# p's loads on a second queue, idle turns and an early table in the prologue; the last unit by hand in two halves and stored in eight pieces

## The chip, the core and the metric

The kernel runs on one core of one Trainium2 chip. The core has five engines that work side by side, each through its own instructions in order: TensorE (PE; its weight loads are shown as PEld), VectorE (DVE), ScalarE (ACT), GpSimd (POOL) and SyncE (SP), which here only issues DMAs. An engine that issues a DMA spends time of its own queue on that, and the 16 DMA engines of the core move the data afterwards. The metric is the time of one execution on the device in microseconds (us); lower is better. TensorE's clock has two levels, 1.2 and 2.4 GHz; the profile shows the granted one as 0.5 or 1.0.

## What is computed

Attention through a packed set of 32 queries, and two feed-forward layers behind it, all in float32:

```python
def sm_attn(qq, kk, vv):
    s = scale * np.matmul(qq, kk.transpose(0, 1, 3, 2))
    s = s - np.max(s, axis=-1, keepdims=True)
    a = np.exp(s)
    a = a / (np.sum(a, axis=-1, keepdims=True) + 1e-09)
    return np.matmul(a, vv)
p_packed = sm_attn(p, k, v)
x = sm_attn(q, p_packed, p_packed)
...
h = x @ w_in;  x = (h * np.cos(h)) @ w_out
...
h = x @ w_in2
P = a[0] + a[1]*h + a[2]*h**2 + a[3]*h**3
Q = 1 + abs(b[0])*abs(h) + abs(b[1])*h**2
out = (P / (Q + 1e-6)) @ w_out2
```

q, k and v are 8 batches x 8 heads x 576 x 64, p is 8 x 8 x 32 x 64; 4608 tokens of 512 features then pass through the two layers with 2048 hidden features.

## The kernel before

The program has three stages.

**The prologue** (up to about 100 us) makes the packed attention. For each batch b, k comes in as one block of 1152 KB (`load_k`, two buffers), v as two pairs of loads (`load_v`, three buffers `vx_p`), and p once: eight loads of 64 KB, one for each head, into `px`, which lies in the third v buffer (line 157). VectorE turns k (`prep`, `prep_ext`, lines 192 to 206) and p (`turn_p`, line 177) so that TensorE can multiply them: `s1` (line 232) makes the scores of a batch in 80 small matmuls, `top` the row maxima on VectorE, `expo` the exponential on ScalarE, `et` turns the result with TensorE by means of `ident` (line 289), `pv` multiplies it by v, and `ppt` and `packed` put it where it is needed. The loop over c (line 566) interleaves these for successive batches, together with the conversion of the first weights (`load_conv`, `conv_in`). The order is written out by hand: `tc.manual_schedule` for ScalarE, VectorE and TensorE (line 153) and for SP (line 156) makes each of these engines keep the order of the program. On SP that is: k's block 0, the eight loads of p, k's block 1, the first block of w_in, the two loads of v's block 0, then k's block 2, which waits until `prep_ext(0)` has freed its buffer, and so on. POOL keeps the scheduler's order; it clears the padding of the v buffers, that of the third one when p has been turned (line 574).

**The first layer** (to 808 us) is ordered by hand too (`slot`, line 912): TensorE makes h (line 726) and y (line 788) in turn, while weights are converted and packed beside it.

**The second layer** works through 144 units (t, f): 9 blocks t of 512 tokens, and 16 groups f of 128 hidden features; they are counted 0 to 143 here. A unit is `mm_h2` (12 matmuls of 512 columns into one PSUM bank, line 1051), `chain2` (line 1078: six passes of ScalarE and six of VectorE over 128 x 512, which form P, and 1/Q by a reciprocal square root, its square and one correction), `finish_g2` (line 1063: the product g is split into a high part on ScalarE, line 1069, and a low part on VectorE, line 1075), and `mm_o` (line 1128: for each of four groups s of 128 tokens three matmuls, high x high, high x low, low x high, into one of four PSUM banks). `mm_o` of a unit comes two units after its h. Here the order is a scheduler's, which works from a simulated timeline. In the last block the outputs of the last two units are added pair by pair (`mm_o(142, 143)`), and `store_last` copies each group of 128 x 512 out of PSUM, one half by ScalarE (line 1119) and one by VectorE (line 1120), and writes two groups in eight DMAs of 64 KB, issued by SP and ScalarE in turn (line 1123): sixteen in all.

Of the kernel before, what the change touches and what calls it, by code (L numbers as in the profile page):

```python
# [9 lines left out]
F32 = mybir.dt.float32  # L10
F32R = mybir.dt.float32r
U32 = mybir.dt.uint32
AF = mybir.ActivationFunctionType
ALU = mybir.AluOpType
# [6 lines left out]
def pack_attention_moe_moe_kernel(  # L21
# [14 lines left out]
    nc = tc.nc  # L36
    B, H, S, D = q.shape
    M = p.shape[2]
    NT, DM = out.shape
# [4 lines left out]
    CB = S // 16  # L44
# [4 lines left out]
    NFC = DFF // 128  # L49
    NKD = DM // 128  # L50
    NDB = D // 32
    scale = 1.0 / math.sqrt(D)
    RND = 1.5 * 2.0 ** 23
    INV2PI = 1.0 / (2.0 * math.pi)
    PASSES = ((0, 0), (0, 1), (1, 0))
# [56 lines left out]
    ident = const.tile([128, 128], F32, name="ident")  # L112
    pick = const.tile([128, 2, 2, M], F32, name="pick")
    par = const.tile([128, 8], F32, name="par")
    coef = const.tile([128, 8], F32, name="coef")
    one = const.tile([128, 1], F32, name="one")
# [3 lines left out]
    QC = 1.0 + 1e-6  # L120

    if True:

        a_p = [ctx.enter_context(tc.tile_pool(name=f"a{i}", bufs=1)) for i in range(2)]
# [3 lines left out]
        wb_p = ctx.enter_context(tc.tile_pool(name="wb", bufs=1, side="right"))  # L128
        cv_p = ctx.enter_context(tc.tile_pool(name="cv", bufs=1, side="right"))
# [4 lines left out]
        ps0 = e0p.enter_context(tc.tile_pool(name="ps0", bufs=1, space=PSUM))  # L134
# [3 lines left out]
        def load_k(b):  # L138
            kx_t[b] = wk.tile([128, CB, D], F32, tag="kx", bufs=2, name="kx")
            nc.sync.dma_start(out=kx_t[b], in_=k[b].rearrange("h (j c) d -> (h j) c d", c=CB))  # L140
# [16 lines left out]
        px = vx_p[2].rearrange("p h c -> p (h c)")[:, 0:B * 2 * D].rearrange("p (b u d) -> p b u d", b=B, u=2)  # L157
# [5 lines left out]
        load_k(0)  # L163
        for h in range(H):
            rg, u = divmod(h, 2)
            nc.sync.dma_start(out=px[32 * rg:32 * rg + 32, :, u], in_=p[:, h].rearrange("b m d -> m b d"))
        load_k(1)
        nc.vector.memset(coef[:, 6:7], RND)
        nc.vector.memset(coef[:, 7:8], math.pi / 2.0)
        nc.vector.memset(par[:, 6:7], QC)  # L170
        qb = par[:, 6:7]
        make_identity(nc, ident)
        nc.vector.tensor_copy(out=pick, in_=ident.rearrange("p (a u m) -> p u a m", a=2, u=2))
        wl = wi_p.tile([128, B * H * 32 + 128], F32, name="wl")
        nc.gpsimd.memset(wl, 0.0)
# [342 lines left out]
        for fq in (0, 2, 1, 3):  # L518
            pool, tag, bufs = (wi_p, "w1i", 2) if fq % 2 else (wb_p, "wb", 8)
# [151 lines left out]
        NB = NT // 512  # L671
        w2_s, x_t, pools = {}, {}, {}
# [8 lines left out]
        def load_x(t):  # L681
            for x in range(2):
                for k2 in range(2):
                    if x and k2:
                        pool, tag, bufs = (const, "pp", 1) if t % 2 else (pools["a"], "x", 1)
                    else:
                        pool, tag, bufs = (pools["b"], f"x{x}{k2}", 1) if t % 2 else (cv_p, "st64", 3)
                    s = pool.tile([128, 2, 512], F32R, tag=tag, bufs=bufs, name=f"x{x}{k2}")
                    nc.sync.dma_start(
                        out=s.bitcast(F32),  # L690
                        in_=yd[x][2 * k2:2 * k2 + 2, :, 512 * t:512 * t + 512].rearrange("k p s -> p k s"),
                    )
                    for i in range(2):
                        x_t[t, x, 2 * k2 + i] = s[:, i]
# [132 lines left out]
        ps1 = ctx.enter_context(tc.tile_pool(name="ps1", bufs=1, space=PSUM, **RW))  # L827
# [207 lines left out]
        psh2 = ctx.enter_context(tc.tile_pool(name="psh2", bufs=1, space=PSUM, **RW))  # L1035
# [6 lines left out]
        slots2 = [(t, f) for t in range(NB) for f in range(NFC)]  # L1042
        h2_t, g2_t, o_t = {}, {}, {}

        def mm_h2(n):
            t, f = slots2[n]
            ps = psh2.tile([128, 512], F32, tag="h2", bufs=4, name="h2")
            i = 0
            for kk in range(NKD):
                for a, c in PASSES:  # L1050
                    nc.tensor.matmul(  # L1051
                        out=ps,
                        lhsT=w2_s[f][:, 0, a, 128 * kk:128 * kk + 128],
                        rhs=x_t[t, c, kk],
                        start=(i == 0),
                        stop=(i == 3 * NKD - 1),
                    )
                    i += 1
            h2_t[n] = ps
# [3 lines left out]
        def finish_g2(n, part):  # L1063
            if n not in gf and n not in g2_t:
                return
            if part == 0:
                gt = gf[n]
                gh = pools["a"].tile([128, 512], F32R, tag="g2h", bufs=3, name="g2h")
                nc.scalar.activation(out=gh, in_=gt, func=AF.Copy)  # L1069
                g2_t[n] = [gh, None]  # L1070
            else:
                gt = gf.pop(n)
                gh = g2_t[n][0]
                gl = pools["a"].tile([128, 512], F32R, tag="g2l", bufs=3, name="g2l")
                nc.vector.tensor_tensor(out=gl, in0=gt, in1=gh.bitcast(F32), op=ALU.subtract)  # L1075
                g2_t[n][1] = gl
# [25 lines left out]
        def store(t, s):  # L1102
            ot = a_p[0].tile([128, DM], F32, tag=("ah", "al")[s % 2], bufs=2, name="ot")
            nc.scalar.activation(out=ot, in_=o_t[s], func=AF.Copy)
            w = 0
            while w < 4:
                b, cc = divmod((512 * t + 128 * s) // 32 + w, C)
                m = min(4 - w, C - cc)
                nc.sync.dma_start(
                    out=out[b * S:b * S + S, :].rearrange("(j c) e -> c j e", c=CB)[2 * cc:2 * (cc + m)],  # L1110
                    in_=ot[32 * w:32 * (w + m), :],
                )
                w += m

        def store_last(t, ss):
            ot = pools["b"].tile([128, 2, DM], F32, tag=f"x0{ss[0] // 2}", bufs=1, name="ol")
            hd = DM // 2
            for i, s in enumerate(ss):
                nc.scalar.activation(out=ot[:, i, 0:hd], in_=o_t[s][:, 0:hd], func=AF.Copy)
                nc.vector.tensor_copy(out=ot[:, i, hd:DM], in_=o_t[s][:, hd:DM])  # L1120
            for w in range(8):
                b, c = divmod((512 * t + 128 * ss[0]) // 16 + w, CB)
                (nc.sync, nc.scalar)[w % 2].dma_start(
                    out=out[b * S:b * S + S, :].rearrange("(j c) e -> j c e", c=CB)[:, c:c + 9:8],
                    in_=ot[16 * w:16 * w + 16],
                )

        def mm_o(*ns):
            for n in ns:
                if slots2[n][1] == 0:  # L1130
                    for s in range(4):
                        o_t[s] = ps1.tile([128, DM], F32, tag=f"y{s}", name=f"o{s}")
            t, f = slots2[ns[-1]]
            ends = t == NB - 1 and f == NFC - 1
            for ss in ((0, 1), (2, 3)) if ends else ((0,), (1,), (2,), (3,)):
                for n in ns:
                    t, f = slots2[n]
                    for s in ss:
                        for i, (a, c) in enumerate(PASSES):
                            nc.tensor.matmul(  # L1140
                                out=o_t[s],
                                lhsT=g2_t[n][a][:, 128 * s:128 * s + 128],
                                rhs=w2_s[f][:, 1, c],
                                start=(f == 0 and i == 0),
                                stop=(f == NFC - 1 and i == 2),
                            )
                if ends:
                    store_last(t, ss)
                elif f == NFC - 1:
                    store(t, ss[0])  # L1150
            for n in ns:
                del g2_t[n]

        for n, (t, f) in enumerate(slots2):
            mm_h2(n)
            chain2(n)
            if f == 2 and 0 < t < NB - 1:
                load_x(t + 1)
            if n >= 2:
                mm_o(n - 2)  # L1160
        finish_g2(len(slots2) - 1, 0)
        finish_g2(len(slots2) - 1, 1)
        mm_o(len(slots2) - 2, len(slots2) - 1)


# [28 lines left out]
```

## Time and profile before

| what | value |
|---|---|
| median of 3 runs (lowest to highest) | 1599.57 us (1599.39 to 1599.61) |
| the profiled execution: its own time | 1599.44 us |
| the profiled execution: span from first to last instruction | 1597.6 us |
| TensorE busy | 1541.5 us, 96% of the span |
| VectorE busy | 1252.9 us, 78% |
| ScalarE busy | 1173.3 us, 73% |
| GpSimd busy | 164.6 us, 10% |
| mean granted clock of TensorE | 0.988 |
| DMA: moved, mean rate | 175.40 MB, 110 GB/s |

All times in what follows are microseconds from the span's start. "Idle before" is the time that an engine stood before a group of instructions, and the arrow names what ended it. In the chain of waits each piece is the work that the next one waited for; "issue" is time in which the engine waited for nothing that the profile shows. A DMA share is the mean busy share of the 16 DMA engines; where packets overlap it can exceed 1.

### The profile page before, as it was taken

What the parts mean: (1) busy time and instruction counts of PE and PEld (TensorE: products, weight loads), DVE (VectorE), ACT (ScalarE), POOL (GpSimd) and SP (SyncE); (2) the same over time, 40 slices, a digit from 0 to 9 for tenths busy, and PEclk for the clock granted to TensorE, in tenths of its full rate; (3) what the DMA queues carried; (4) which work ended last, traced back from release to release, by engine and by line L of the source; (5) the groups of instructions that cost most, each with busy time, mean ns of one, the idle gap of its engine ahead of it and who ended that gap; (6) DMA issues with size and microseconds to landing.
All of it is one profiled execution on the core that took longest, in us unless ns stands there. A gap on an engine that the chain in (4) does not pass through costs nothing.

```text
span 1597.6 us, 26583 instructions
## 1 busy us (share of the span) xinstructions
PE 1541.5 (96%) x10096; PEld 1328.5 (83%) x10096; DVE 1252.9 (78%) x1897; ACT 1173.3 (73%) x1979; POOL 164.6 (10%) x126
## 2 busy tenths in 40 slices
PE   5789999999999999999999999999999999999997
PEld 3455679999999999999988888888888888888886
DVE  6768787777878787779668888888888888889886
ACT  3566776777777777777677778777787778788875
POOL 1124331020202020203100000000000000000000
PEclk8889999999999999999999999999999999999999
DMA  9747773434434443345970102010111010020000
GB/s 353 242 172 255 231 241 124 125 124 125 128 121 132 120 137 120 126 146 177 312 263 31 49 1 74 7 54 26 54 27 53 27 53 27 5 75 1 27 1 26
DMA packets 98863, 175.40 MB, mean 110 GB/s; under 512 B 11568, under 2 KB 44848, under 8 KB 97712
## 3 DMA queue, kind: packets, MB, share of 16 engines
q1 hardware_dynamic: 98352, 173.19, 32.9%
q8 instruction: 79, 1.29, 0.3%
q10 hardware_dynamic: 384, 0.52, 0.1%
q14 instruction: 48, 0.39, 0.1%
HBM read 113.31 MB, written 60.36 MB: 109 GB/s over the span
## 4 chain that ended last, share of the span: by engine, by line
PE 87%; DVE 5%; ACT 3%; DMA 2%; issue 2%; SPq 0%; POOL 0%; DVEq 0%; POOLq 0%; ACTq 0%
PE h L1051 25%; PE o L1140 24%; PE y L788 22%; PE h L726 11%; PE s L221 2%; PE w L383 1%; DMA vx<-in_v_dram 1%; DVE cvf L86 1%; PE w L357 1%; DVE cvf L91 1%; ACT r L757 1%; ACT r L756 0%; PE pv L302 0%; DVE kT L197 0%; DMA st<-in_moe_w_out_dram 0%
## 5 line engine op out<-in xcount | busy, mean ns | idle before, releaser
L788 PE MATMUL y<-gh,w1o 128*128 128x288 f32 x2048 | 433.9, 297 | 0.9 <-DVE yl L71 0.9
L1051 PE MATMUL h<-x,w 128*128 128x512 f32 x1728 | 406.0, 389 | 0.0
L1051 PEld LDWEIGHTS h<-x,w 128*128 128x128 f32 x1728 | 324.2, 188 | 67.2
L788 PEld LDWEIGHTS y<-gh,w1o 128*128 128x128 f32 x2048 | 334.6, 188 | 6.9 <-issue 5.2
L788 PE MATMUL y<-gl,w1o 128*128 128x288 f32 x1024 | 302.3, 295 | 2.8 <-DVE gl L71 2.5
L1140 PE MATMUL o<-w,g2h 128*128 128x512 f32 x1152 | 292.9, 389 | 1.4 <-ACT g2h L1069 1.4
L1140 PEld LDWEIGHTS o<-w,g2h 128*128 128x128 f32 x1152 | 216.1, 188 | 47.0 <-ACT g2h L1069 2.2
L726 PE MATMUL h<-ah,wq 128*128 128x288 f32 x1024 | 227.4, 298 | 2.6 <-DVE g L758 1.8
L1086 ACT ACTIVATE sq<-h 128x512 f32<-128x512 f32 x144 | 87.4, 607 | 162.3 <-PE h L1051 162.3
L788 PEld LDWEIGHTS y<-gl,w1o 128*128 128x128 f32 x1024 | 192.1, 188 | 9.5 <-DVE gl L71 5.6
L726 PEld LDWEIGHTS h<-ah,wq 128*128 128x128 f32 x1024 | 170.6, 188 | 13.8 <-issue 9.7
L758 DVE SCALAR_TENSOR_TENSOR g<-h,r 128x576 f32<-128x576 f32 x128 | 96.9, 757 | 100.2 <-ACT r L757 100.0
L1140 PE MATMUL o<-w,g2l 128*128 128x512 f32 x576 | 162.1, 389 | 0.0
L726 PE MATMUL h<-al,wq 128*128 128x288 f32 x512 | 150.5, 294 | 0.0
L750 ACT ACTIVATE u<-h,coef 128x576 f32<-128x576 f32 x128 | 94.0, 734 | 70.5 <-PE h L726 69.9
L756 ACT ACTIVATE r<-r 128x576 f32<-128x576 f32 x128 | 87.8, 686 | 78.4 <-DVE r L751 78.3
L1097 DVE SCALAR_TENSOR_TENSOR ab<-ab,y 128x512 f32<-128x512 f32 x144 | 99.3, 689 | 55.6 <-ACT y L1094 55.6
L751 DVE SCALAR_TENSOR_TENSOR r<-u,h 128x576 f32<-128x576 f32 x128 | 95.1, 743 | 48.8 <-ACT u L750 47.4
L1075 DVE TENSOR_TENSOR g2l<-c,g2h 128x512 fp32r<-128x512 f32 x144 | 99.1, 688 | 37.0 <-ACT g2h L1069 36.8
L1140 PEld LDWEIGHTS o<-w,g2l 128*128 128x128 f32 x576 | 108.1, 188 | 22.5
L1089 ACT ACTIVATE c<-h,coef 128x512 f32<-128x512 f32 x144 | 114.0, 792 | 4.6 <-DVE g2l L1075 4.6
L1088 DVE SCALAR_TENSOR_TENSOR ab<-sq,coef,ab 128x512 f32<-128x512 f32 x144 | 107.5, 746 | 12.5 <-ACT ab L1087 12.5
(117 smaller groups left out, 2269.2 us busy)
## 6 DMA issues: line engine op xcount, KB each, us to landing
x<-yd SPq DMA_DIRECT2D x36, 512.0 KB
st<-in_moe_w_in_dram SPq DMA_DIRECT2D x32, 512.0 KB
st<-in_moe_w_out_dram SPq DMA_DIRECT2D x32, 512.0 KB
w<-w2d SPq DMA_DIRECT2D x64, 256.0 KB
wq<-wd SPq DMA_DIRECT2D x56, 256.0 KB
wd<-wev SPq DMA_DIRECT2D x48, 256.0 KB
kx<-in_k_dram SPq DMA_DIRECT2D x8, 1152.0 KB
qx<-in_q_dram SPq DMA_DIRECT2D x16, 576.0 KB
```

The lines of the kernel that those rows point to most:

```text
L726: last_h[0] = nc.tensor.matmul(out=ps[:, u, 0:HS], lhsT=wq[:, g, a, o:o + 128], rhs=a_t[b, g][c][:, hf], start=(i == 0), stop=(i == 3 * G ...
L750: nc.scalar.activation(out=u, in_=ph, func=AF.Identity, bias=coef[:, 6:7])
L751: nc.vector.scalar_tensor_tensor(out=r, in0=u, scalar=RND, in1=ph, op0=ALU.subtract, op1=ALU.subtract)
L756: nc.scalar.activation(out=r, in_=r, func=AF.Abs)
L758: nc.vector.scalar_tensor_tensor(out=gt, in0=ph, scalar=2.0 * math.pi, in1=r, op0=ALU.mult, op1=ALU.mult)
L788: nc.tensor.matmul(out=y_t[d][:, 0:HS], lhsT=w1o_s[f // 4][a][:, f % 4, 128 * d:128 * d + 128], rhs=gs[c][:, u], start=(first and u == 0 a ...
L1051: nc.tensor.matmul(out=ps, lhsT=w2_s[f][:, 0, a, 128 * kk:128 * kk + 128], rhs=x_t[t, c, kk], start=(i == 0), stop=(i == 3 * NKD - 1),)
L1075: nc.vector.tensor_tensor(out=gl, in0=gt, in1=gh.bitcast(F32), op=ALU.subtract)
L1088: nc.vector.scalar_tensor_tensor(out=ab, in0=sq, scalar=coef[:, 5:6], in1=ab, op0=ALU.mult, op1=ALU.add)
L1089: nc.scalar.activation(out=c1, in_=ph, func=AF.Identity, scale=coef[:, 3:4], bias=coef[:, 2:3])
L1097: nc.vector.scalar_tensor_tensor(out=ab, in0=ab, scalar=QC, in1=y0, op0=ALU.add, op1=ALU.mult)
L1140: nc.tensor.matmul(out=o_t[s], lhsT=g2_t[n][a][:, 128 * s:128 * s + 128], rhs=w2_s[f][:, 1, c], start=(f == 0 and i == 0), stop=(f == NFC ...
```

## The change

In the prologue the eight loads of p are issued by ScalarE and no longer by SP. ScalarE then runs one exponential over a 128 x 1 tile, which loads the table of the exponential at that point. TensorE turns `ident` twenty times into a PSUM tile that nothing reads. In the second layer the last unit leaves the loop and is written out by hand (`last_unit`): its h in two halves of 256 tokens in the same PSUM bank, and each half through the whole chain of ScalarE and VectorE in a fixed order, the split of unit 142 between them. `mm_o` takes one unit at a time again. The result of the last block is copied into one tile and written in eight DMAs of 128 KB, four from each queue.

```diff
         load_k(0)
         for h in range(H):
             rg, u = divmod(h, 2)
-            nc.sync.dma_start(out=px[32 * rg:32 * rg + 32, :, u], in_=p[:, h].rearrange("b m d -> m b d"))
+            nc.scalar.dma_start(out=px[32 * rg:32 * rg + 32, :, u], in_=p[:, h].rearrange("b m d -> m b d"))
         load_k(1)
         nc.vector.memset(coef[:, 6:7], RND)
...
         qb = par[:, 6:7]
+        nc.scalar.activation(out=one, in_=coef[:, 6:7], func=AF.Exp, scale=0.0)
         make_identity(nc, ident)
+        warm = ps0.tile([128, 1024], F32, tag="et", name="warm")
+        for i in range(20):
+            nc.tensor.transpose(warm[:, 0:128], ident, ident)
         nc.vector.tensor_copy(out=pick, in_=ident.rearrange("p (a u m) -> p u a m", a=2, u=2))
...
+        def o_step(n, s):
+            t, f = slots2[n]
+            for i, (a, c) in enumerate(PASSES):
+                nc.tensor.matmul(
+                    out=o_t[s],
+                    lhsT=g2_t[n][a][:, 128 * s:128 * s + 128],
+                    rhs=w2_s[f][:, 1, c],
+                    start=(f == 0 and i == 0),
+                    stop=(f == NFC - 1 and i == 2),
+                )
...
+        def last_unit():
+            n = len(slots2) - 1
+            t, f = slots2[n]
+            ps = psh2.tile([128, 512], F32, tag="h2", bufs=4, name="h2")
+            hw = [slice(256 * i, 256 * i + 256) for i in range(2)]
+            for w in hw:
+                for kk in range(NKD):
+                    for i, (a, c) in enumerate(PASSES):
+                        nc.tensor.matmul(
+                            out=ps[:, w],
...
+            def a1(w):
+                act(out=sq[:, w], in_=ps[:, w], func=AF.Square)
+                act(out=ab[:, w], in_=ps[:, w], func=AF.Abs, scale=coef[:, 4:5])
+                vec.scalar_tensor_tensor(
+                    out=ab[:, w], in0=sq[:, w], scalar=coef[:, 5:6], in1=ab[:, w], op0=ALU.mult, op1=ALU.add
+                )
+
+            def a2(w):
+                act(out=c1[:, w], in_=ps[:, w], func=AF.Identity, scale=coef[:, 3:4], bias=coef[:, 2:3])
+                act(out=c0[:, w], in_=ps[:, w], func=AF.Identity, scale=coef[:, 1:2], bias=coef[:, 0:1])
+                vec.tensor_tensor(out=c1[:, w], in0=c1[:, w], in1=sq[:, w], op=ALU.mult)
+                vec.tensor_tensor(out=c1[:, w], in0=c1[:, w], in1=c0[:, w], op=ALU.add)
+
+            def a3(w):
+                act(out=y0[:, w], in_=ab[:, w], func=AF.Abs_reciprocal_sqrt, bias=qb)
+                act(out=y0[:, w], in_=y0[:, w], func=AF.Square)
+                vec.scalar_tensor_tensor(
+                    out=ab[:, w], in0=ab[:, w], scalar=QC, in1=y0[:, w], op0=ALU.add, op1=ALU.mult
+                )
+                vec.tensor_tensor(out=c1[:, w], in0=c1[:, w], in1=y0[:, w], op=ALU.mult)
+                vec.scalar_tensor_tensor(
+                    out=c1[:, w], in0=ab[:, w], scalar=2.0, in1=c1[:, w], op0=ALU.subtract, op1=ALU.mult
+                )
+
+            def a4(w):
+                act(out=gh[:, w], in_=c1[:, w], func=AF.Copy)
+                vec.tensor_tensor(out=gl[:, w], in0=c1[:, w], in1=gh[:, w].bitcast(F32), op=ALU.subtract)
+
+            a1(hw[0])
+            a2(hw[0])
+            a3(hw[0])
+            finish_g2(n - 1, 0)
+            finish_g2(n - 1, 1)
+            a1(hw[1])
+            a2(hw[1])
+            a4(hw[0])
+            a3(hw[1])
+            a4(hw[1])
+            g2_t[n] = (gh, gl)
+            mm_o(n - 2)
+            mm_o(n - 1)
+            ot = wb_p.tile([128, 4, DM], F32, tag="wb", bufs=8, name="ol")
             hd = DM // 2
...
+            for s in range(4):
+                o_step(n, s)
+                nc.scalar.activation(out=ot[:, s, 0:hd], in_=o_t[s][:, 0:hd], func=AF.Copy)
+                nc.vector.tensor_copy(out=ot[:, s, hd:DM], in_=o_t[s][:, hd:DM])
             for w in range(8):
...
                 (nc.sync, nc.scalar)[w % 2].dma_start(
-                    out=out[b * S:b * S + S, :].rearrange("(j c) e -> j c e", c=CB)[:, c:c + 9:8],
+                    out=out[b * S:b * S + S, :].rearrange("(j c) e -> j c e", c=CB)[:, c:c + 25:8],
                     in_=ot[16 * w:16 * w + 16],
                 )
...
-        for n, (t, f) in enumerate(slots2):
+        for n, (t, f) in enumerate(slots2[:-1]):
             mm_h2(n)
             chain2(n)
...
             if n >= 2:
                 mm_o(n - 2)
-        finish_g2(len(slots2) - 1, 0)
-        finish_g2(len(slots2) - 1, 1)
-        mm_o(len(slots2) - 2, len(slots2) - 1)
+        with tc.manual_schedule(
+            engines={mybir.EngineType.Activation, mybir.EngineType.DVE, mybir.EngineType.PE}
+        ):
+            last_unit()
```

## Rows read from the trace of the kernel before

**Rows 1.** The page's chain that ended last, by line.
```profile
PE h L1051 25%; PE o L1140 24%; PE y L788 22%; PE h L726 11%; PE s L221 2%; PE w L383 1%; DMA vx<-in_v_dram 1%; DVE cvf L86 1%; PE w L357 1%; DVE cvf L91 1%; ACT r L757 1%; ACT r L756 0%; PE pv L302 0%; DVE kT L197 0%; DMA st<-in_moe_w_out_dram 0%
```
**Rows 2.** The chain of waits, 0 to 50 us: start us, us, what.
```profile
4.37 3.81 DMA vx<-in_p_dram
...
8.64 0.40 DVE kT L204
...
9.29 4.11 PE s L221 x60
...
15.22 2.29 DVE kT L197 x2
...
47.97 1.80 issue
```
**Rows 3.** The timeline, 0 to 40 us: start us, us, engine line op out<-in xcount.
```profile
1.20 5.45 SPq L166 DMA_DIRECT2D vx<-in_p_dram  x8
...
3.65 0.29 POOL masks.py:199 TENSOR_SCALAR_AFFINE_SELECT ident<-ident 128x128 f32<-128x128 f32 x1
...
6.35 2.37 DVE L197 STREAM_TRANSPOSE kT<-kx 128x1024 f32<-128x1024 f32 x2 [2.14 <-DMA kx<-in_k_dram]
...
14.45 1.28 ACT L268 ACT_TABLE_LOAD   x1 [14.45 <-DVE nb L251]
...
21.91 1.33 PE L289 MATMUL et<-ident,E 128*128 128x128 f32 x5
...
26.04 2.33 PE L221 MATMUL s<-kT,pp 32*32 32x512 f32 x64
```
**Rows 4.** SP's waits, 0 to 12 us: total us, times, longest us.
```profile
SPq L166 <- DMA kx<-in_k_dram: 1.5, 1, 1.5
```
**Rows 5.** Windows of 0.5 us: busy PE, PEld, DVE, ACT, POOL; PEclk, DMA share, GB/s.
```profile
3.00:3.50 0.50, 0.00 (x0) 0.00 (x0) 0.00 (x0) 0.00 (x0) 0.50 (x1) 1.00 0.94 387
6.00:6.50 0.50, 0.00 (x0) 0.00 (x0) 0.15 (x1) 0.00 (x0) 0.00 (x0) 1.00 1.28 279
```
**Rows 6.** Waits of all engines, 0 to 50 us: total us, times, longest us.
```profile
DVE kT L197 <- DMA kx<-in_k_dram: 2.9, 2, 2.1
...
PE pv L302 <- DMA vx<-in_v_dram: 1.3, 1, 1.3
```
**Rows 7.** Windows of 2 us, columns as in rows 5.
```profile
16.00:18.00 2.00, 0.35 (x8) 0.34 (x16) 1.97 (x4) 2.00 (x9) 0.00 (x0) 0.67 0.96 397
...
22.00:24.00 2.00, 1.24 (x5) 0.83 (x5) 1.93 (x5) 1.09 (x5) 0.00 (x0) 0.62 1.06 429
```
**Rows 8.** The timeline, 1560 to 1600 us, columns as in rows 3.
```profile
1579.92 0.60 ACT L1086 ACTIVATE sq<-h 128x512 f32<-128x512 f32 x1 [1.13 <-PE h L1051]
1580.15 0.69 DVE L1099 SCALAR_TENSOR_TENSOR c<-ab,c 128x512 f32<-128x512 f32 x1
...
1583.01 2.11 PE L1140 MATMUL o<-w,g2h 128*128 128x512 f32 x8 [0.40 <-ACT g2h L1069]
...
1588.97 1.08 PE L1140 MATMUL o<-w,g2l 128*128 128x512 f32 x4
...
1590.59 4.14 SPq L1123 DMA_DIRECT2D out_dram<-ol  x8
```
**Rows 9.** Groups by line and shape, 1578 to 1598 us: busy us, mean ns | idle before.
```profile
L1140 PE MATMUL o<-w,g2l 128*128 128x512 f32 x15 | 4.4, 389 | 0.0
...
L1075 DVE TENSOR_TENSOR g2l<-c,g2h 128x512 fp32r<-128x512 f32 x3 | 2.1, 688 | 0.7 <-ACT g2h L1069 0.7
...
L1120 DVE COPY ol<-o 128x256 f32<-128x256 f32 x4 | 1.4, 417 | 2.1 <-ACT ol L1119 2.1
...
L1119 ACT ACTIVATE ol<-o 128x256 f32<-128x256 f32 x4 | 1.2, 390 | 2.5 <-PE o L1140 2.5
```
**Rows 10.** Windows of 1 us: the tail and a store in mid-run; columns as in rows 5.
```profile
1592.00:1593.00 1.00, 0.00 (x0) 0.00 (x0) 0.00 (x0) 0.00 (x0) 0.00 (x0) 1.00 0.93 238
...
1511.00:1512.00 1.00, 1.00 (x6) 0.81 (x6) 0.90 (x3) 1.00 (x3) 0.00 (x0) 1.00 0.52 203
```

More of the change, by code (lines that the diff above doesn't have):

```diff
@@ L1113, in store @@
                 w += m
-        def store_last(t, ss):
-            ot = pools["b"].tile([128, 2, DM], F32, tag=f"x0{ss[0] // 2}", bufs=1, name="ol")
+        def o_step(n, s):
[8 more added lines that the diff above has]
+                )
@@ new lines, in mm_o @@
+        def mm_o(n):
+            t, f = slots2[n]
+            if f == 0:
+                for s in range(4):
+                    o_t[s] = ps1.tile([128, DM], F32, tag=f"y{s}", name=f"o{s}")
+            for s in range(4):
+                o_step(n, s)
+                if f == NFC - 1:
+                    store(t, s)
+            del g2_t[n]
+        def last_unit():
+            n = len(slots2) - 1
+            t, f = slots2[n]
+            ps = psh2.tile([128, 512], F32, tag="h2", bufs=4, name="h2")
[5 more added lines that the diff above has]
+                            out=ps[:, w],
+                            lhsT=w2_s[f][:, 0, a, 128 * kk:128 * kk + 128],
+                            rhs=x_t[t, c, kk][:, w],
+                            start=(kk == 0 and i == 0),
+                            stop=(kk == NKD - 1 and i == 2),
+                        )
+            sq, c1 = (
+                pool.tile([128, 512], F32, tag=tg, bufs=3 if tg == "cvf" else 2, name=nm)
+                for pool, tg, nm in ((cv_p, "cvf", "sq"), (a_p[1], "ah", "c1"))
+            )
+            c0, y0 = (pools["a"].tile([128, 512], F32, tag=nm, bufs=2, name=nm) for nm in ("c0", "y0"))
+            ab = a_p[1].tile([128, 512], F32, tag="al", bufs=2, name="ab")
+            gh, gl = (pools["a"].tile([128, 512], F32R, tag=x, bufs=3, name=x) for x in ("g2h", "g2l"))
+            act, vec = nc.scalar.activation, nc.vector
+            def a1(w):
[14 more added lines that the diff above has]
+                    out=ab[:, w], in0=ab[:, w], scalar=QC, in1=y0[:, w], op0=ALU.add, op1=ALU.mult
+                )
+                vec.tensor_tensor(out=c1[:, w], in0=c1[:, w], in1=y0[:, w], op=ALU.mult)
+                vec.scalar_tensor_tensor(
+                    out=c1[:, w], in0=ab[:, w], scalar=2.0, in1=c1[:, w], op0=ALU.subtract, op1=ALU.mult
+                )
+            def a4(w):
[15 more added lines that the diff above has]
+            ot = wb_p.tile([128, 4, DM], F32, tag="wb", bufs=8, name="ol")
@@ L1117, in store_last @@
             hd = DM // 2
-            for i, s in enumerate(ss):
-                nc.scalar.activation(out=ot[:, i, 0:hd], in_=o_t[s][:, 0:hd], func=AF.Copy)
-                nc.vector.tensor_copy(out=ot[:, i, hd:DM], in_=o_t[s][:, hd:DM])
+            for s in range(4):
+                o_step(n, s)
+                nc.scalar.activation(out=ot[:, s, 0:hd], in_=o_t[s][:, 0:hd], func=AF.Copy)
+                nc.vector.tensor_copy(out=ot[:, s, hd:DM], in_=o_t[s][:, hd:DM])
             for w in range(8):
-                b, c = divmod((512 * t + 128 * ss[0]) // 16 + w, CB)
+                b, c = divmod(512 * t // 16 + w, CB)
@@ L1123, in store_last @@
                 (nc.sync, nc.scalar)[w % 2].dma_start(
-                    out=out[b * S:b * S + S, :].rearrange("(j c) e -> j c e", c=CB)[:, c:c + 9:8],
+                    out=out[b * S:b * S + S, :].rearrange("(j c) e -> j c e", c=CB)[:, c:c + 25:8],
                     in_=ot[16 * w:16 * w + 16],
                 )
[L1128 to L1152, printed above, removed]
```

## The prediction

> **What bounds it now.** Read first the page's chain by line [rows 1]: nearly all of the span is TensorE at lines 1051, 1140, 788 and 726, which follow one another without a pause. A microsecond won or lost before or behind that middle therefore reaches the end one for one, and the middle itself is not touched. So I read two edges: the chain of waits and the timeline up to 50 us, and the timeline of the last 20 us.
>
> In the prologue the reader is to see two arms that meet at 9.29 us, where the first scores start [rows 2]. One arm is k's first block: its load goes out first and VectorE turns it from 6.35 us on, without a pause until 9.04 [rows 2, 3]. The other is p: eight loads, of which the last is late [rows 3] because it waits 1.5 us for k's first load to land [rows 4]. It is the ninth DMA of the program, and the first had not landed: I read this as eight in flight at most. p is there at 8.18 [rows 2], 0.86 before VectorE is free for it. So p is not what the first scores wait for; k's 2.7 us of turning is.
>
> **The change at the front.** It takes eight issues from SP's queue (5.45 us, [rows 3]) and puts them on ScalarE's, which has nothing to do before 14.45 [rows 3], so eight issues of 0.5 cost nothing there; with nothing to hide them they would cost 4. Past them move forward on SP: k's second block, the first block of w_in and both loads of the first v, all some 5.4 us earlier. k's third block stays where it was, since it waits for k's first buffer (VectorE, 9.04). The loads brought forward need about 2.3 MB that so far moved after 8.5 us; before that, the engines moved k's first block at 387 GB/s and then p at 279 GB/s with a share of over 1 [rows 5], so p's 0.52 MB is worth 1.9 us of all DMA engines although it is small.
>
> *The wait.* Two queues issue side by side at some 0.5 us each (5.45 less the wait of 1.5, over 8), so the first eight DMAs are four of SP's (k, k, w_in, v) and four of p's, and the ninth to thirteenth, among them p's last four loads or so, each wait for the one eight places ahead. One of those is k's second block. Its 1152 KB take 3.0 us at 387 GB/s behind the first, which was in at 6.35; p's first five loads, in the same engines, take 5/8 of 1.9, that is 1.2. So it lands at 10.6; the waiting p load and one more are issued (1.0), and p's last landed 1.5 after its issue had ended (6.65 to 8.18). p is complete at 13.1, turned 0.2 later, and the first scores start at 13.3 in place of 9.29: **+4.0**. Bounds: +0 to +1.9 if no p load waits (then p's packets only push back k's first block by up to 1.9), +4.9 if the load waited for is the first of w_in, 512 KB and 1.3 us behind. I take +4.0, since the order of issue makes k's second block the one in that place.
>
> Queued behind the waiting p loads on ScalarE is only the table's load: it ends by 13, still before the first exponential. VectorE waits for p with its turn, and then does everything behind it in the same order. POOL's memset of the third v buffer and SP's third v load wait for p's turn and go out later too; two blocks of v are read before that one, and they cover it. If they did not, the third unit's product with v would be what is late.
>
> *What comes back.* With the DMA engines never idle from 1.5 us on, and compute later, the two waits for loads fall away: 0.8 for k's fourth block (2.9 less the first 2.1) and 1.3 for v [rows 6]. TensorE's 1.80 of "issue" at 47.97 [rows 2] has no releaser; I count half, 0.9. That is −3.0, bounds 0 and −3.9.
>
> *The table.* Its load is 1.28 us on ScalarE [rows 3]. Beside it VectorE reduces and turns k until 17.51, and the chain goes through VectorE there [rows 2], so I count −0.1. If VectorE were earlier by more than that, the table would be the next thing late, at up to 1.28.
>
> *The idle turns.* ident is ready at 3.94 [rows 3]. Five turns at the low clock take 1.33 [rows 3], twenty at most 5.3: over by 9.3, no later than the scores can start, so they delay nothing. They can pay by raising the clock: the first 64 score matmuls took 4.11, the same work at 26.04 took 2.33 [rows 2, 3], −1.8. The granted clock did rise to 2.4 GHz right behind five turns (22 to 24 us), and fell to 1.2 between 16 and 18 after TensorE had stood since 13.4 [rows 7]. From 9.3 to 13.3 it stands 4.0 us, longer than it did by the fall (a mean of 0.67 puts that at 16.7). So 0 here, bounds −1.8 and 0.
>
> The Trainium skill (TensorE: Matmul & The Clock Gate, Part 4: PE-mode transpose) says that transposes do not count towards the full clock. The rise at 22 to 24 speaks against it, though scores ran just before. By the rule the turns are worth 0 in any case, which is rival B.
>
> Front: 4.0 − 3.0 − 0.1 = **+0.9**.
>
> **The change at the end.** Before, ScalarE starts the last unit at 1579.92 when its h is done [rows 8]. Afterwards h comes in 24 matmuls of 256 columns in place of 12 of 512. Both engines of a copy out of one PSUM tile took turns, VectorE waiting for ScalarE [rows 9], so I let ScalarE wait for both halves: same start. An earlier one would gain nothing: VectorE is busy with unit 142 until 1580.84 [rows 8]. Half-wide steps cost 0.39 on ScalarE and 0.42 on VectorE [rows 9]; bounds are these and the full widths (0.69 on VectorE). For the first half: ab on VectorE to 1581.3; reciprocal root and square, which wait for c1 and c0 on ScalarE, to 1582.4; three on VectorE to 1583.6; and only then, since the order is now by hand, unit 142's low part at 0.69 [rows 9]: 1584.35. Queued behind it is TensorE: its third matmul of unit 142 now needs that low part, where before eight others ran first from 1583.01 [rows 8]. From there 22 matmuls remain at 0.23 (four take 1.08 [rows 8], of which the last stands 0.39 [rows 9]): 1589.5, against 1590.05. The second half's low part is ready at 1587.9, just as it is needed. Then ScalarE's and VectorE's last copies, 0.39 + 0.42 and 0.1 between: first store at 1590.47, against 1590.59 [rows 8]: −0.1, bounds −0.6 and +0.6.
>
> From the first store to the span's end are 7.0 us. Sixteen issues become eight, four on each queue, no longer held by eight in flight, but each carries 128 KB, and all wait for the last copy. The 1.05 MB moved at 238 GB/s with a share of 0.93 [rows 10], 4.4 us in all; a store of 256 KB in mid-run went at 203 with a share of 0.52 [rows 10], that is 390 when full, or 2.7 us. I take 3.3, since half of the issues remain: −1.1, bounds 0 and −1.7. End: **−1.2**.
>
> **Sum.** The profiled execution took 1599.44 (span 1597.6). +0.9 − 1.2 = −0.3 gives 1599.1; the median of the runs is 0.13 higher, so 1599.3.
>
> **Rivals.**
> *A, p is not held back.* If the eight are not counted over both queues, or the order spares p, the first scores wait only for k's first block, delayed by half of p's 1.9: 10.2, right behind the turns, at 2.33: they end 0.9 earlier. With 0.8, 1.3 and 0.1: −3.1, end −1.2: 1595.3. For it: five us of SP's queue were indeed spent on p. Against: [rows 4].
> *B, A without the clock.* The same, but the turns do not raise it: +0.9 − 2.2 − 1.2 = −2.5, 1597.1. Against it is [rows 7]. By the rule that the Trainium skill states (TensorE: Matmul & The Clock Gate, Part 4) it would be this.
> *C, slower.* p's last load waits behind w_in's first block in ScalarE's queue: +4.9, and the prologue, whose steps are mostly VectorE's, gives nothing back: 4.9 − 0.1 − 1.2 = +3.6, 1603.2. It decides as soon as the delay that is left at 50 us exceeds 4.4. For it: only 2.1 us of waits up to 50 us name loads.
> The Trainium skill (DMA: Bandwidth & Descriptors, Issuing engines are not separate DMA queues) says that a second issuing engine saves only issue time, as the transfers share the engines. No row here shows two queues loading at once; by it, A loses the full 1.9 in place of 0.9, 1596.3.
>
> **Numbers.** Forecast 0.55 (its own range 1597 to 1602), A 0.22, B 0.08, C 0.15. What a measurement can tell from no change is about 0.2%, 3.2 us. Faster by more: most of A and a little of the forecast, 0.27. Slower by more: most of C, 0.13. Within: 0.60. The range runs from A to just short of C: 1595.0 to 1602.8.
>
> **What would show it.** Right: first scores near 13.3, 4.1 us long, k's second block landed before p's last load goes out; no wait for k or v between 26 and 44; last matmul near 1589.5; 5.9 us from first store to the end. Wrong: first scores at or before 10.2 (A, and B if they take 4.1), a delay still whole at 50 us (C), or a gap between units in the middle.

## The result, and the profile after

The changed kernel takes **1607.7 us** (median of 6 runs, 1605.14 to 1612.11), the kernel before 1599.48 beside it (6 runs, 1597.06 to 1600.74): the ratio is 1.0058, with a 95% interval of 1.0045 to 1.0070. It is slower, by 8.2 us in the medians, where I had forecast 0.2 less, and outside the range. The profiled execution is the shortest of the six: 1605.14 us, with a span of 1603.4 against 1597.6; what is read from it below is 2.4 us less than the loss of the medians. One execution of the experiments, e5's first, ran in a slow state (1928.78 us at a mean granted clock of 0.75) and enters no comparison.

The chain by line of the page after shows the same middle as [rows 1]; the load of p is new among the small pieces:

```profile
PE h L1055 24%; PE o L1122 24%; PE y L792 22%; PE h L730 11%; PE s L225 1%; PE w L387 1%; DMA wd<-wev 1%; DMA vx<-in_p_dram 1%; DVE kT L201 1%; DVE cvf L86 1%; PE w L361 1%; ACT E L272 1%; DVE cvf L91 0%; DVE r L755 0%; ACT r L761 0%
```

The chain of waits after, 0 to 50 us (start us, us, what), answers to [rows 2]:

```profile
1.69 11.34 DMA vx<-in_p_dram
13.05 6.47 DMA vx<-in_p_dram
...
19.75 0.32 DVE pp L182
...
20.12 3.79 PE s L225 x58
...
25.74 2.29 DVE kT L201 x2
```

In place of one load of 3.81 us there are two, end to end, of 11.34 and 6.47: a load of p issued at 1.69 lands at 13.05, and one that could only go out then lands at 19.5. From there on the chain is arithmetic alone: up to 112 us it holds no other load.

The timeline after, 0 to 30 us, answers to [rows 3]:

```profile
0.73 12.77 ACTq L166 DMA_DIRECT2D vx<-in_p_dram  x8
0.73 0.93 SPq L140 DMA_DIRECT2D kx<-in_k_dram  x2
...
1.71 0.47 SPq L492 DMA_DIRECT2D st<-in_moe_w_in_dram  x1
2.22 5.37 SPq L149 DMA_DIRECT2D vx<-in_v_dram  x2
...
4.00 4.53 PE L176 MATMUL warm<-ident 128*128 128x128 f32 x20 [4.00 <-POOL ident masks.py:199]
6.91 2.37 DVE L201 STREAM_TRANSPOSE kT<-kx 128x1024 f32<-128x1024 f32 x2 [2.70 <-DMA kx<-in_k_dram]
...
13.54 1.28 ACT L172 ACT_TABLE_LOAD   x1 [13.54 <-DMA vx<-in_p_dram]
...
19.75 1.30 DVE L182 STREAM_TRANSPOSE pp<-vx 128x128 f32<-128x128 f32 x2 [10.14 <-DMA vx<-in_p_dram]
...
20.12 3.85 PE L225 MATMUL s<-kT,pp 32*32 32x512 f32 x64 [11.59 <-DVE pp L182]
```

k's first block is turned 0.56 later than before (6.91 for 6.35) and done by 9.6; then VectorE stands for 10.1 us and TensorE for 11.6, both for p. The eight issues on ScalarE's queue take 12.77 us, most of it waiting, and the table's load, behind them, comes at 13.54. SP's queue waits too, for the same loads (SP's waits after, 0 to 24 us: total us, times, longest us):

```profile
SPq L149 <- DMA vx<-in_p_dram: 5.2, 3, 3.3
SPq L140 <- DMA st<-in_moe_w_in_dram: 4.3, 1, 4.3
SPq L149 <- DMA kx<-in_k_dram: 3.8, 1, 3.8
```

So the places in flight are counted over both queues, as I had read [rows 4]. What I had not seen is why the loads that hold these places were so slow. The DMA view counts packets by queue (queue, packets, MB, share of 16 engines); SP's loads are in q1 and ScalarE's in q10. After, 4 to 6 us and 6 to 8 us:

```profile
q1 hardware_dynamic: 96, 0.79, 94.4%
q10 hardware_dynamic: 95, 0.02, 5.3%
...
q1 hardware_dynamic: 98, 0.85, 99.9%
q10 hardware_dynamic: 98, 0.02, 5.1%
```

Before, 6 to 8 us, when k's first block was in and almost everything that moved was p:

```profile
q1 hardware_dynamic: 1480, 0.45, 111.5%
```

**The two queues take turns packet by packet.** SP's packets here are of some 8 KB on average (0.79 MB over 96), p's of 256 bytes (0.52 MB in 2048). With equal turns p moves 98 packets in 2 us, where alone it moved some 1480. Until 10 us the counts stay equal (148 to 151 from 8 to 10); they rise when SP comes to v, whose packets are smaller (453 to 554 from 10 to 12). The Trainium skill (DMA: Bandwidth & Descriptors, Queues, rings and completion order) says that each DMA engine serves the queues that have work in turn, a packet at a time. These counts agree, one for one in what the profile counts as a packet.

Where the time went, as the start of the 64 score matmuls of each batch, and of the square of unit 142 at the other end of the span (all from timelines; e1 and e6 are experiments below):

| us | batch 0 | 1 | 2 | 3 | 4 | 5 | 6 | 7 | unit 142 |
|---|---|---|---|---|---|---|---|---|---|
| before | 9.29 | 17.65 | 26.04 | 35.00 | 44.05 | 57.19 | 68.82 | 78.13 | 1574.48 |
| after | 20.12 | 28.16 | 36.47 | 44.24 | 53.51 | 64.32 | 75.92 | 86.44 | 1579.74 |
| later by | 10.83 | 10.51 | 10.43 | 9.24 | 9.46 | 7.13 | 7.10 | 8.31 | 5.26 |
| e1: after, p on SP | 9.28 | 15.80 | 25.97 | 34.22 | 43.03 | 54.52 | 67.97 | 77.31 | 1573.31 |
| e6: after, p on GpSimd | 14.09 | 20.61 | 28.91 | 36.45 | 45.79 | 56.66 | 68.34 | 78.28 | 1572.57 |

The start loses 10.83 us, of which 5.26 are left at unit 142. The end adds 0.54, and 5.8 is the difference of the spans.

**The end.** The timeline after, 1579 to 1604 us, answers to [rows 8]:

```profile
1588.44 0.73 PE L1122 MATMUL o<-w,g2h 128*128 128x512 f32 x2 [0.37 <-ACT g2h L1073]
...
1589.77 0.50 PE L1122 MATMUL o<-w,g2l 128*128 128x512 f32 x1 [0.60 <-DVE g2l L1079]
...
1594.67 0.39 PE L1122 MATMUL o<-w,g2l 128*128 128x512 f32 x1
...
1595.51 0.42 DVE L1211 COPY ol<-o 128x256 f32<-128x256 f32 x1 [0.25 <-ACT ol L1210]
1595.96 3.09 SPq L1214 DMA_DIRECT2D out_dram<-ol  x4
1595.97 3.10 ACTq L1214 DMA_DIRECT2D out_dram<-ol  x4
```

Less the 5.26, TensorE's third matmul of unit 142 starts at 1584.51, behind VectorE's low part as forecast (1584.35); the last matmul ends at 1589.80 (before 1590.05), and the first store goes out at 1590.70 (before 1590.59). From there to the end are 7.44 us, before 7.0. The windows of that tail (columns as in [rows 5]):

```profile
1596.00:1597.00 1.00, 0.00 (x0) 0.00 (x0) 0.00 (x0) 0.00 (x0) 0.00 (x0) 1.00 0.16 27
...
1598.00:1599.00 1.00, 0.00 (x0) 0.00 (x0) 0.00 (x0) 0.00 (x0) 0.00 (x0) 1.00 1.17 246
...
1600.00:1601.00 1.00, 0.00 (x0) 0.00 (x0) 0.00 (x0) 0.00 (x0) 0.00 (x0) 0.59 1.07 287
...
1602.00:1603.40 1.40, 0.00 (x0) 0.00 (x0) 0.00 (x0) 0.00 (x0) 0.00 (x0) 0.50 0.00 0
```

### The profile page after: what moved, and what is told of

It is laid out like the page before. It is cut to its first block, busy times and chain, and to the rows that moved or that the text cites. A ratio compares the mean times of both kernels' runs of the same rounds, so it can differ in the third digit from the quotient of the medians.

```text
span 1603.4 us, 26647 instructions
## 1 busy us (share of the span) xinstructions
PE 1542.0 (96%) x10128; PEld 1330.2 (83%) x10128; DVE 1253.0 (78%) x1904; ACT 1175.8 (73%) x1987; POOL 165.2 (10%) x126
## 4 chain that ended last, share of the span: by engine, by line
PE 85%; DVE 5%; ACT 4%; DMA 3%; issue 2%; SPq 0%; POOL 0%; ACTq 0%; DVEq 0%
PE h L1055 24%; PE o L1122 24%; PE y L792 22%; PE h L730 11%; PE s L225 1%; PE w L387 1%; DMA wd<-wev 1%; DMA vx<-in_p_dram 1%; DVE kT L201 1%; DVE cvf L86 1%; PE w L361 1%; ACT E L272 1%; DVE cvf L91 0%; DVE r L755 0%; ACT r L761 0%
```

## The experiments

The theory after this trace: p on ScalarE's queue alone costs the time, because it moves beside SP's loads; the rest of the change is worth about nothing. The rivals: that the end is slower, that ScalarE's queue is slow by itself, and that only the waiting for places in flight counts.

**e1: p's loads back on SP**, all else as in the changed kernel.

```diff
-            nc.scalar.dma_start(out=px[32 * rg:32 * rg + 32, :, u], ...
+            nc.sync.dma_start(out=px[32 * rg:32 * rg + 32, :, u], ...
```

> The changed kernel with p's eight loads back on SP's queue; table, turns and the new end stay. Theory (p beside SP's loads lands late, and that is all of the front's loss): first scores again at 9 to 10 us, and within 1.5 us of the kernel before. If the turns raise the clock the first scores take 2.3 in place of 4.1 and it is 0 to 2 us faster than before. Rival (the table's load, the turns or the new order by hand at the end cost the time): still 4 us or more slower than before.

Measured: 1598.36 us (10 runs), ratio to before 0.9998 (0.9989 to 1.0007). The whole loss is gone.

**e2: the kernel before, with p's loads on ScalarE** and nothing else.

```diff
-            nc.sync.dma_start(out=px[32 * rg:32 * rg + 32, :, u], ...
+            nc.scalar.dma_start(out=px[32 * rg:32 * rg + 32, :, u], ...
```

> The kernel before with p's eight loads on ScalarE's queue, nothing else. Theory: first scores at 18 to 21 us, and 5 to 8 us slower than before at the end, since only about half of the 10.8 is made good later. Rival (the turns, which end long before the scores, or the table behind p on ScalarE share in the loss): less than 3 us slower than before.

Measured: 1609.82 us (4 runs), 1.0071 (1.0056 to 1.0086): 11.3 us more than before, and more than expected. Its chain of waits, 0 to 50 us, has the same two loads, the second still longer than after:

```profile
1.69 10.93 DMA vx<-in_p_dram
12.63 8.80 DMA vx<-in_p_dram
```

Scores start at 22.03 in place of 9.29, and 11.79 of the 12.74 are left at unit 142 (1586.27). Of its four runs (1607.75 to 1611.79) the profiled one, 1611.13, is among the longer, where the profiled one of after is the shortest; so the two traces are further apart than the medians, which are 11.3 and 8.2 above the kernel before. With e1, this one line is shown to be the cause.

**e3: the kernel before, with the new end** (`o_step`, `mm_o`, `last_unit` and its eight stores, as in the change).

> The kernel before with the new last unit and the eight stores, nothing else. Theory: last matmul 0.2 to 0.3 us earlier against the start of unit 142, tail 0.4 us longer: +0.5 us in sum, between -0.5 and +1. Rival (the end loses more than the profile shows, some 3 us in the median): +2 to +4.

Measured: 1599.41 us, 1.0006 (0.9996 to 1.0015). Its first store goes out at 1590.64 and the span ends at 1598.0, so the tail is 7.36, again no shorter than the 7.0 before.

**e4: the kernel before, with the early table and the twenty turns**; **e9: with the turns alone**.

```diff
         qb = par[:, 6:7]
+        nc.scalar.activation(out=one, in_=coef[:, 6:7], func=AF.Exp, scale=0.0)
         make_identity(nc, ident)
+        warm = ps0.tile([128, 1024], F32, tag="et", name="warm")
+        for i in range(20):
+            nc.tensor.transpose(warm[:, 0:128], ident, ident)
```

> The kernel before with the table's early load and the twenty turns, nothing else. Theory: the turns are over at 8.5, the first scores start at 9.3, right behind them, at 2.4 GHz: 2.3 us long in place of 4.1, the table saves at most 0.1: 0 to 2 us faster than before. Rival (turns do not count towards the full clock): first scores 4.1 us long, no difference over 0.5 us.

> The kernel before with the twenty turns alone; the table's load stays where it was. If the turns are what made e4_turns_table's scores short, the first scores start near 9.2 and take 2.3 us here too, the table's load stands behind them as before (14 to 15), and the time is that of e4_turns_table or up to 1.3 us more: 1597 to 1599. If the early table had a part in it, the scores take about 4.1.

Measured: e4 1597.10 us, 0.9993 (0.9983 to 1.0002); e9 1598.41 us, 0.9996 (0.9987 to 1.0006). The two can't be told apart, nor from before. The timeline of e4, 0 to 30 us:

```profile
4.00 3.88 PE L176 MATMUL warm<-ident 128*128 128x128 f32 x20 [4.00 <-POOL ident masks.py:199]
...
9.15 2.33 PE L225 MATMUL s<-kT,pp 32*32 32x512 f32 x64 [1.28 <-DVE pp L182]
...
15.67 4.22 PE L225 MATMUL s<-kT,pp 32*32 32x512 f32 x64 [4.20 <-DVE kT L201]
18.76 2.37 DVE L201 STREAM_TRANSPOSE kT<-kx 128x1024 f32<-128x1024 f32 x2 [1.41 <-DMA kx<-in_k_dram]
```

The turns do what they are there for: right behind them the first scores take 2.33 us in place of 4.13, and the second scores start at 15.67 in place of 17.65. But the third turn of k now waits 1.41 for its load, and the third scores start at 26.01, where they did before (26.04). So the early start runs into the loads: the third turn is left 0.63 ahead (18.76 for 19.39). The rest goes on TensorE, where the two groups ahead of the third scores take 1.06 and 1.29 us in place of 0.77 each (granted clock 0.53 from 24 to 26 us, before 1.00). The loads are seen in the chain of waits of e1 too, 0 to 115 us, whose first scores start at 9.28 and take 2.33 as well:

```profile
16.01 11.74 DMA kx<-in_k_dram
```

k's fourth block is issued at 16.01 and lands at 27.75; in the kernel before it goes out at 17.86 and is in at 28.02. Issued 1.85 earlier, it lands 0.27 earlier, and what came earlier has to wait for that.

**e5: SP held back.** The changed kernel, but k's second block, and with it all that SP issues behind it, goes out only when the last load of p is in.

```diff
-            nc.scalar.dma_start(out=px[32 * rg:32 * rg + 32, :, u], ...
-        load_k(1)
+            last_p = nc.scalar.dma_start(out=px[32 * rg:32 * rg + 32, :, u], ...
+        tc.add_manual_dep(load_k(1).ins, last_p.ins.name, ...)
```

> The changed kernel, but SP issues k's second block, and with it all its later loads, only when p's last load has landed: ScalarE's queue moves p beside k's first block alone. Theory (p's 256-byte pieces get a small part of the DMA engines while SP's loads stand beside them): p complete by 8 to 11 us, first scores at 9.5 to 11.5, and the whole within 2.5 us of the kernel before. Rival (loads issued by ScalarE are slow as such, or held by one another): p's first load again takes 7 us or more and the scores start after 13.

Measured: 1600.54 us (median of nine runs), 1.0008 (0.9999 to 1.0017). For a profile I ran the same kernel once more:

> The kernel of e5_held once more, for a profile of the whole span: p complete near 9.3, scores near 9.8, 3.6 us long; k's second block, held until p is in, lands near 13 and is what the second scores wait for, w_in and v come some 4 us later than in the changed kernel. By the share theory the delay at unit 142 is then at most 1 us against the kernel before; by the theory that ScalarE's queue is slow as such p would again be late, near 15.

Measured: 1600.21 us, span 1598.4. The chain of waits, 0 to 50 us, and the DMA view, 4 to 6 and 6 to 8 us:

```profile
3.98 4.11 DMA vx<-in_p_dram
...
9.42 4.11 PE s L230 x61
...
18.01 11.66 DMA kx<-in_k_dram
```

```profile
q1 hardware_dynamic: 78, 0.57, 69.8%
q10 hardware_dynamic: 507, 0.12, 27.8%
...
q10 hardware_dynamic: 1548, 0.37, 84.1%
```

While the rest of k's first block moves, p gets its turns, one for one until 5 us (41 packets of each queue from 3 to 4 us); once SP's queue is empty it moves 1548 packets in 2 us, as fast as on SP's queue before, and is in at 8.1. So ScalarE's queue isn't slow: p is slow beside a queue of large packets. Scores start at 9.42 (I had expected 9.8). They took 4.14, though the same twenty turns ran just before them.

**e6: p's loads issued by GpSimd.**

```diff
-            nc.scalar.dma_start(out=px[32 * rg:32 * rg + 32, :, u], ...
+            nc.gpsimd.dma_start(out=px[32 * rg:32 * rg + 32, :, u], ...
```

> The changed kernel with p's loads issued by GpSimd: none of them waits for a load eight places ahead, but SP's loads stand beside them as in the changed kernel (ident comes after the issues, so the turns are later). Theory (the share): p is still late, first scores after 15 us. Rival (the wait for a place among eight in flight costs the time): p complete by 11, first scores before 12.

Measured: 1597.95 us in one execution, span 1596.2. Its timeline, 0 to 32 us:

```profile
1.57 4.74 POOL L166 DMA_DIRECT2D vx<-in_p_dram  x8
...
8.87 2.36 DVE L201 STREAM_TRANSPOSE kT<-kx 128x1024 f32<-128x1024 f32 x2
...
13.73 1.30 DVE L182 STREAM_TRANSPOSE pp<-vx 128x128 f32<-128x128 f32 x2 [2.17 <-DMA vx<-in_p_dram]
...
14.09 2.33 PE L225 MATMUL s<-kT,pp 32*32 32x512 f32 x64 [1.11 <-DVE pp L182]
```

Neither expectation holds: p is in at 13.6, later than on one queue and earlier than after. It doesn't separate the sharing from the waiting as cleanly as I had meant, for here p moves as 256 packets of 2 KB in place of 2048 of 256 bytes (from 10 to 12 us 99 of them beside 106 of SP's, turn for turn again). k's first block is turned late (8.87) because GpSimd makes `ident` behind p, and VectorE waits 7.8 for that first. What it does show is the worth of a late start: scores 4.8 later than before, and unit 142 is 1.9 earlier (1572.57 for 1574.48), in one execution of each.

**e7: p's loads on both queues in turn**, in the kernel before with the turns and the table; SP's four ahead of k's second block.

```diff
-            nc.sync.dma_start(out=px[32 * rg:32 * rg + 32, :, u], ...
+            (nc.scalar if h % 2 == 0 else nc.sync).dma_start(out=px[32 * rg:32 * rg + 32, :, u], ...
```

> The kernel before with the early table and the turns, and p's loads in turn on ScalarE's and SP's queue, SP's four directly behind k's first block and ahead of k's second. Theory: ScalarE's four have only k's first block and p's other half beside them; p complete by 8 to 9, k's first block at most 0.7 later, first scores at 9.2 to 10, and SP is free 2 us sooner: between 1 us slower and 2 us faster than the kernel before. Rival (any p load on ScalarE's queue is late): scores after 11, slower by 2 or more.

Measured: 1598.23 us, 0.9997 (0.9988 to 1.0007). Scores start at 9.38. Four loads of p on ScalarE's queue do no harm here, where p's other half is what SP's queue holds behind k's first block. The DMA view of this run, 6 to 8 us, has p's packets of 256 bytes in both queues:

```profile
q1 hardware_dynamic: 746, 0.18, 40.2%
q10 hardware_dynamic: 689, 0.16, 37.4%
```

With packets of one size the two queues get nearly equal shares of the bytes; from 3 to 4 us, with k's block in SP's queue, the packets were 43 to 43 and the bytes 0.40 to 0.01 MB. So the share goes by the size of the packets, and neither queue goes first here.

**e8: sixteen stores again**, in the kernel of e1: SP's eight go out as soon as two groups are copied, ScalarE's eight after the other two.

```diff
-            for w in range(8):
...
+                if s % 2:
+                    for w in range(8):
...
+                        (nc.sync, nc.scalar)[s // 2].dma_start(
...
+                            in_=ot[16 * w:16 * w + 16, s - 1:s + 1],
+                        )
```

> The changed kernel with p's loads back on SP and sixteen stores again in the new end: eight of 64 KB by SP as soon as two of the four groups are copied, eight by ScalarE for the other two. Theory (the new end's tail was 0.4 us longer because all eight large stores wait for the last copy): the first store goes out 1.2 to 1.4 us before the last matmul's copy, and the time from the last matmul to the end falls from 8.3 to some 7: 1 to 2 us faster than the kernel before. Rival (the tail is bound by the 1 MB at 240 GB/s whenever it starts, or by ScalarE's issues): no more than 0.5 us faster.

Measured: 1598.17 us (11 runs), 0.9991 (0.9983 to 1.0000). Its SP and ScalarE timelines, 1585 to 1597 us:

```profile
1588.48 3.81 SPq L1215 DMA_DIRECT2D out_dram<-ol  x8
...
1588.97 0.38 ACT L1210 ACTIVATE ol<-o 128x256 f32<-128x256 f32 x1 [0.29 <-PE o L1122]
1589.85 4.41 ACTq L1215 DMA_DIRECT2D out_dram<-ol  x8
```

From the last copy's start to the end of the span are 7.73 us here (1588.97 to 1596.7), after 8.31 (1595.09 to 1603.4): half of the stores under way beside the last matmuls are worth 0.6, and their number does no harm. The 1 to 2 us that I expected of it are not shown. This and e4, 0.9 and 1.4 us under the kernel before by their medians, have the lowest ratios of all; neither is told from it by 0.2%, so no version here beats it for certain.

## Why the prediction was wrong, step by step

**The wait (+4.0, measured +10.8) is the step that failed.** Its first half was right: the loads are counted over both queues, eight in flight, and p's later loads wait for a place. But I priced them as waiting for k's second block (in by 10.6), and took p's own first loads to land beside it at their share of bytes ("5/8 of 1.9"). The first landed about 7.3 us and the third 11.3 us after its issue, since a queue's share goes by packets: 256 bytes of p for some 8 KB of SP's. The last loads waited for p's own first ones, and p was complete at 19.6 in place of 13.1. Both bounds rested on rows of one queue; no row of before showed two queues loading at once, and I said so only where I cited the Trainium skill (DMA: Bandwidth & Descriptors, Issuing engines are not separate DMA queues). By its rule a second issuing engine changes only the time of issue. In this trace it changed who gets the engines: p was in 11.4 us later (19.6 for 8.2), and SP's large loads, which had been queued behind it, were in the engines first.

How much of the 10.8 is the waiting for places, and how much the turns, was not separated. The turns alone hold the first load for 7.3 us and the third for 11.3, and neither waited for a place. Between 13 and 16 us, when the last loads had just gone out, p's queue moved only 55 packets (27 and 28), so by estimate the waiting added 2 to 3 us.

**What comes back (−3.0, measured −5.6 in this execution).** Right in kind, and larger in the one execution that has a trace. In the median, if its start and its end were those of the trace, about 3.2 came back (10.83 and 0.54, less 8.2), which is near the forecast. In the kernel before, the chain of waits from 26 to 50 us holds two loads of v end to end, where I had counted only the 1.3 us that TensorE stood for them:

```profile
26.76 7.18 DMA vx<-in_v_dram
...
34.00 9.26 DMA vx<-in_v_dram
```

The windows from 26 to 28 us (columns as in [rows 5]), before and after, show the same by the DMA share:

```profile
26.00:28.00 2.00, 2.00 (x60) 0.85 (x53) 1.18 (x3) 1.07 (x3) 0.65 (x1) 1.00 1.03 430
```

```profile
26.00:28.00 2.00, 0.00 (x0) 0.00 (x0) 2.00 (x3) 1.62 (x7) 0.00 (x0) 0.66 0.17 68
```

Up to 43 us the kernel before, and e1 up to 28, are paced by loads, so a later or an earlier start of the scores is little felt. In after the loads are ahead of the compute, and the share falls to 0.17. e6 uses up that slack: its chain holds no load behind p's, 4.8 us of delay cost nothing, and further microseconds count. From e6 to after scores start 6.03 later, and unit 142 is 7.17 later. That also fits the twenty turns, which bring 1.8 and end as nothing. Two parts of what came back are not as I had priced them. The 1.80 of "issue", of which I counted half, did not go with the later start but with the turns: e2 keeps 1.33 of it and e3 1.17, and no kernel with the turns has it at that place (five of the eight pause 0.23 to 1.67 in the product with v instead; after does not). And the delay fell from 6.67 at the first layer's first h (115.57 for 108.90) to 5.26 at the second layer's first square (809.64 for 804.38), in the middle that I held untouched; why is not shown. How much comes back is not steady: next to nothing did in e2 (11.79 of 12.74 left), and the six runs after spread over 7 us, with a mean granted clock of 0.990 in the shortest and 0.984 in the longest. I did not find what decides that.

**The table (−0.1).** Its load came at 13.54, before the first exponential (24.98), and held up nothing else. Right in kind; 0.1 us is too little for these runs to show.

**The idle turns (0, bounds −1.8 and 0).** The size was right for the end, and the reason I gave was right for after: TensorE stood 11.6 us behind them, and the scores took 3.85. In e1, e4, e6, e7 and e9 scores right behind the turns took 2.33; in e8 and e10, with turns at the same time as in e1 (4.00 to 8.53), 4.04 and 4.14. In the kernel before the same scores take 2.33 where the column of the granted clock reads 1.00 (26 to 28 us) and 4.33 where it falls to 0.50 (17.65 to 22 us). So the turns can raise the clock to 2.4 GHz, but not in every execution, and what decides it stays open. That column reads 1.00 from 9 to 13 us in e1 and in e8 alike; only the durations tell. The rule that transposes do not count towards the full clock (the Trainium skill, TensorE: Matmul & The Clock Gate, Part 4: PE-mode transpose) does not hold in the first five, where TensorE did nothing but these turns before; the rows call them MATMUL and do not show whether they ran in the mode that the page means.

**The end (−1.2, measured +0.54).** Its matmul part holds: the third matmul of unit 142 at 1584.51 (1584.35), the last at 1589.80 (1589.5, as 22 matmuls took 0.24 each and not 0.23), the first store at 1590.70 (1590.47). The term that was mis-sized is the tail, 5.9 forecast and 7.44 measured, 1.5 of the 1.7 us that the end is off by. I priced the transfer by a store in mid-run, 390 GB/s when full; here the windows show 246 and 287 GB/s with a share over 1, and the four issues of each queue took 3.09 us, 0.77 each, where eight took 4.14 ([rows 8]), 0.52 each. Twice the bytes in half the stores were no faster, and all of them waited for the last copy.

**The rivals.** C had the sign and its deciding point (a delay over 4.4 at 50 us; it was 9.5), but neither its place (w_in's first block) nor its size (+3.6). A and B are excluded by the scores at 20.12.

## What to carry to other kernels

Before a load is moved to another queue, look at the size of its packets and at what the other queue will be moving at that moment: the queues take turns packet by packet, so a load of small packets that others wait for belongs ahead of the large ones in the same queue, or in a second queue only while the first is empty. And read from the chain of waits how far the stage around it is paced by loads: within that slack a late or an early start is little felt (e6, e1), and beyond it most of it is (after, e2).

## What I had not expected of the hardware

- A 64 KB load that was issued at 1.69 us landed 11.34 us later, with 256-byte packets in one queue and packets of some 8 KB in the other, one for one (95 to 96, 98 to 98 in 2 us).
- The same twenty turns, from 4.00 to 8.53, left TensorE at either level: scores of 2.33 us (e1) and of 4.04 us (e8), starting within 0.06 us of each other.
- Eight stores of 128 KB took no less time from the first issue to the end than sixteen of 64 KB: 7.44 and 7.36 (e3) against 7.0.
